# Down projection of a decode step: fourteen rows in row form, fourteen as stationary blocks, five loads in place of four

## The chip, the cores and the metric

The kernel runs on one core of one Trainium2 chip. The metric is the device time of one execution in microseconds (us). Every number of a "time" below is such a device time; numbers with a place in the execution ("at 404.6") are counted from the start of the profiled span, which is about 1.8 us shorter than the device time. PE is TensorE, DVE is VectorE, ACT is ScalarE, PSUM is the accumulator memory that PE writes.

## The reference

One token goes through attention over a cache of 65,536 positions and then through a gated feed-forward layer. Only the last product matters here.

```python
def _B_ref(x, w_gate, w_up, w_down):
    return (_gelu(x @ w_gate) * (x @ w_up)) @ w_down     # F = 3584, D = 1024, one row of x

h  = x + _A_ref(_layernorm(x), ...)                      # attention, [cut]
h2 = h + _B_ref(_layernorm(h), w_gate, w_up, w_down)
```

The down projection multiplies a vector of 3584 values by a 3584 x 1024 matrix of bf16 (7.3 MB). The kernel splits the 3584 as 128 partitions x 28, so there are 28 "rows" c, each of 128 x 1024 weights. 1024 outputs are 8 x 128 (index j, then p).

## The kernel before

Two ways of forming the products stand in it. In **row form** the activations are stationary, padded to 32 columns, and the weights stream by, 512 columns at a time. The sums come out as rows, in four bands of a PSUM bank. They then need a copy to SBUF (`d_r`) and a product with a selector (`cp_sum`) that turns them into columns. In **masked form** the stationary operand has 8 columns, of which only column j is not zero, and 128 weight columns stream by; each product then adds into row j of an 8 x 128 result, which needs no turning.

```python
def pair_mm(bank, stat, w2, c, first, last):                   # row form
    for s in range(DS):                                        # DS = 2
        g = 2 * s + c % 2
        nc.tensor.matmul(bank[32 * g:32 * g + 32, :], lhsT=stat, rhs=w2[:, s * 512:(s + 1) * 512],
                         start=first, stop=last, tile_position=(0, 32 * g))

def cp_sum(row, add, name):                                    # rows to columns, plus add
    ps = ps_t.tile([P, 4, DS], F32, name=name + "_ps", tag="T")
    for b in range(4):
        nc.tensor.matmul(ps[:, b, :], lhsT=row[:, b * P:(b + 1) * P], rhs=hsel[:], start=True, stop=True)
    # [cut: one DVE add of ps and add]

# [cut: attention, out projection, layer norm, gate and up projections, which leave act_bf]
sizes = [FC // 2, FC // 2 - 5, 4, 1]                           # 14, 9, 4, 1 rows
NW = sizes[0] + sizes[1]                                       # 23 rows in row form
actz = padded(rows, act_bf[:, 0:NW], NW, "actz")
# [cut: actm, the masked stationary operands, filled by 8 copies]

c0 = 0
for sz in sizes[:2]:
    wv = load(wd_v[:, c0:c0 + sz, :], "wd_sb")
    for cc in range(sz):
        c = c0 + cc
        pair_mm(d_ps, actz[:, c, :], wv[:, cc, :], c, c < 2, c + 2 >= NW)
    c0 += sz
d_r = rows.tile([P, 512], F32, name="d_r")
nc.vector.tensor_copy(out=d_r[:], in_=d_ps[:])
wv = load(wd_v[:, c0:c0 + sizes[2], :], "wd_sb")
masked_rows(wv, c0, True, False)                               # 4 rows x 8 masked products
c0 += sizes[2]
hd_cp = cp_sum(d_r, h_cp, "hd_cp")
nc.tensor.matmul(o_ps[:], lhsT=hd_cp[:], rhs=ident_f[:], start=False, stop=False)
wv = load(wd_v[:, c0:c0 + sizes[3], :], "wd_sb")
masked_rows(wv, c0, False, True)                               # the last row
o_row = rows.tile([DC, P], BF16, name="o_row")
nc.vector.tensor_copy(out=o_row[:], in_=o_ps[:])
nc.sync.dma_start(out=out[0, 0].rearrange("(c p) -> c p", p=P), in_=o_row[:])
```

## Time and profile before

| | before |
|---|---|
| median of 3 executions | 419.05 us (418.85 to 419.56) |
| the profiled execution | 417.21 us, span 415.4 |
| read from HBM | 173.02 MB, 416 GB/s over the span |
| start of the down projection's products (`d_ps`) | 399.13 |
| end of the last weight packets | 407.4 |
| end of `o_row`, after which only the store is left | 413.33 |

The page of the profile cuts the span into 40 equal slices. The rows below are the granted clock of TensorE in tenths of full speed, the busy share of the DMA engines in tenths, and what they moved. The load stream is full until the last slice.

```profile
span 415.4 us, 6247 instructions
...
PEclk9997999999899999599999967999999586658866
DMA  8999999999999999999999999999999999999990
GB/s 354 429 429 437 420 447 420 437 433 428 443 420 402 431 439 428 433 422 432 437 428 429 434 432 428 420 422 437 431 429 438 423 440 426 430 436 423 434 409 32
```

The chain of waits, in order of time (start, length, what): followed back from the last instruction, what released each step.

```profile
376.18 28.39 DMA wd_sb<-in_B_w_down_dram
...
404.61 1.59 PE d_ps L358 x18
...
406.22 0.70 DVE d_r L471
...
406.96 1.86 PE hd_cp_ps L387 x8
408.82 3.50 PE o_ps L459 x32
412.33 0.23 PE o_ps L476 x2
412.56 0.46 PE o_ps L459 x8
...
413.05 0.28 DVE o_row L480
```

From the landing of the 9-row load on, PE and DVE work one after the other for 8.8 us without waiting for a load. The row form's closing (copy and column sum, 2.6 us) stands in the middle of it, and the 40 masked products behind that.

Stretches of half a microsecond of the same execution: length, PE busy (instructions), granted clock, DMA share, GB/s. The count in brackets includes instructions that only reach into the stretch, so length over count is not the distance between two starts.

```profile
401.50:402.00 0.50, 0.50 (x8) 0.50 0.83 356
402.00:402.50 0.50, 0.22 (x4) 1.00 1.15 492
...
405.50:406.00 0.50, 0.50 (x6) 0.50 0.39 160
...
407.00:407.50 0.50, 0.50 (x3) 0.50 0.04 16
```

The loads are over at about 407.4, six microseconds ahead of the end of `o_row`. The clock is 1.0 in one stretch of about 3.4 us (402.0 to 405.4) and 0.5 on either side.

### The profile page before, as it was taken

How to read it: one execution, taken by the hardware profiler on the slowest of the kernel's cores; microseconds unless marked ns; L12 is line 12 of the kernel's file. 1: busy time of each engine (PE TensorE's matmuls, PEld its weight loads, DVE VectorE, ACT ScalarE, POOL GpSimd, SP SyncE). 2: the span in 40 equal slices, each digit the busy share in tenths (PEclk: the TensorE clock that was granted, in tenths of full speed). 3: DMA queues.
4: the chain of work that ended last, by engine and by line, in shares of the span. 5: the costliest groups of instructions: out<-in, count | busy, mean ns of one | idle time of the engine just before them, and what ended most of it. 6: DMA issues, size and time to landing. Idle time of an engine off the chain costs nothing.

```text
span 415.4 us, 6247 instructions
## 1 busy us (share of the span) xinstructions
PE 302.2 (73%) x2652; PEld 196.9 (47%) x2652; DVE 168.2 (40%) x298; ACT 168.1 (40%) x281; POOL 5.7 (1%) x17
## 2 busy tenths in 40 slices
PE   0458989888788986597988929888986563575536
PEld 0227656564465664464565517465564231352215
DVE  0213565656356455354465526455465000011101
ACT  0014757545755653734565544365562700000000
POOL 1100000000000000000000000000000002000000
PEclk9997999999899999599999967999999586658866
DMA  8999999999999999999999999999999999999990
GB/s 354 429 429 437 420 447 420 437 433 428 443 420 402 431 439 428 433 422 432 437 428 429 434 432 428 420 422 437 431 429 438 423 440 426 430 436 423 434 409 32
DMA packets 6684, 173.43 MB, mean 417 GB/s; under 512 B 896, under 2 KB 896, under 8 KB 1152
## 3 DMA queue, kind: packets, MB, share of 16 engines
q1 hardware_dynamic: 6496, 173.02, 97.2%
q8 instruction: 21, 0.34, 0.3%
q14 instruction: 7, 0.06, 0.0%
q10 hardware_dynamic: 160, 0.00, 0.0%
HBM read 173.02 MB, written 0.00 MB: 416 GB/s over the span
## 4 chain that ended last, share of the span: by engine, by line
PE 51%; DMA 20%; DVE 13%; issue 8%; ACT 6%; POOL 1%; SPq 0%; POOLq 0%; ACTq 0%; DVEq 0%
PE kt_ps L220 27%; PE qk_ps L245 11%; DMA k_sb<-in_A_k_cache_dram 7%; DMA wd_sb<-in_B_w_down_dram 7%; DMA v_sb<-in_A_v_cache_dram 6%; DVE sc_sb L256 5%; PE acc_ps L300 5%; PE sct_ps L253 4%; ACT pT L283 4%; DVE mx L257 3%; DVE kt_sb L227 3%; ACT qk_sb L250 2%; PE wg_ps L160 1%; PE o_ps L459 1%; PE o_ps L316 1%
## 5 line engine op out<-in xcount | busy, mean ns | idle before, releaser
L220 PE MATMUL kt_ps<-ident_f,k_sb 128*128 128x128 f32 x1024 | 149.2, 289 | 15.9 <-DVE kt_sb L227 13.0
L225 ACT COPY kt_sb<-kt_ps 128x1024 bf16<-128x1024 bf16 x116 | 116.4, 1013 | 91.7 <-PE kt_ps L220 61.6
L220 PEld LDWEIGHTS kt_ps<-ident_f,k_sb 128*128 128x128 f32 x1024 | 118.2, 147 | 53.9 <-issue 21.2
L227 DVE COPY kt_sb<-kt_ps 128x1024 bf16<-128x1024 bf16 x140 | 94.8, 687 | 74.5 <-PE qk_ps L245 41.9
L245 PE MATMUL qk_ps<-kt_sb,qsel 128*32 128x512 bf16 x512 | 65.4, 397 | 7.3 <-DVE kt_sb L227 7.3
L256 DVE COPY sc_sb<-sct_ps 128x512 f32<-128x512 f32 x32 | 34.2, 1067 | 47.3 <-PE sct_ps L253 45.0
L283 ACT ACTIVATE pT<-sc_sb,nbias 128x256 bf16<-128x256 f32 x64 | 31.5, 494 | 20.4 <-DVE nbias L275 20.4
L300 PE MATMUL acc_ps<-v_sb,pT 128*32 128x512 bf16 x512 | 33.7, 408 | 2.8 <-DMA v_sb<-in_A_v_cache_dram 2.8
L250 ACT COPY qk_sb<-qk_ps 128x512 f32<-128x512 f32 x32 | 18.9, 590 | 24.8 <-PE qk_ps L245 16.5
L245 PEld LDWEIGHTS <-qsel 128*32 128x32 bf16 x512 | 15.1, 94 | 26.7 <-issue 24.4
L253 PE MATMUL sct_ps<-ident_f,qk_sb 128*128 128x128 f32 x128 | 20.4, 283 | 8.6 <-ACT qk_sb L250 8.6
L300 PEld LDWEIGHTS <-pT 128*32 128x32 bf16 x512 | 14.3, 101 | 18.0 <-issue 6.2
L257 DVE TENSOR_REDUCE mx<-sc_sb 128x8 f32<-128x512 f32 x32 | 22.0, 686 | 1.0
L253 PEld LDWEIGHTS sct_ps<-ident_f,qk_sb 128*128 128x128 f32 x128 | 14.7, 143 | 13.6 <-ACT qk_sb L250 13.6
L167 ACT COPY wg_ev<-wg_ps 96x512 f32<-96x512 f32 x1 | 0.6, 582 | 45.6 <-PE wg_ps L160 45.6
L309 PE MATMUL l_ps<-lpart,ones_f 128*128 128x8 f32 x16 | 3.7, 306 | 15.6 <-ACT pT L283 15.6
L358 PE MATMUL at_ps<-wo_sb,o2z 128*32 128x512 bf16 x64 | 7.2, 629 | 9.4 <-DMA wo_sb<-in_A_wo_dram 9.4
L160 PEld LDWEIGHTS <-hnz 128*32 128x32 bf16 x112 | 5.0, 125 | 15.3 <-issue 13.3
L167 ACT ACT_TABLE_LOAD x1 | 1.3, 1283 | 26.9 <-DVE q_ev L165 26.9
L160 PE MATMUL wu_ps<-wu_sb,hnz 128*32 128x512 bf16 x56 | 6.7, 597 | 7.4 <-DMA wu_sb<-in_B_w_up_dram 7.4
L283 ACT ACTIVATION_READ_ACCUMULATOR pT<-sc_sb,nbias 128x1 f32 x64 | 12.0, 187 | 0.0
L309 PEld LDWEIGHTS l_ps<-lpart,ones_f 128*128 128x128 f32 x16 | 3.0, 234 | 17.8 <-ACT pT L283 17.4
(126 smaller groups left out, 103.0 us busy)
## 6 DMA issues: line engine op xcount, KB each, us to landing
k_sb<-in_A_k_cache_dram SPq DMA_DIRECT2D x16, 4096.0 KB, 26.6
v_sb<-in_A_v_cache_dram SPq DMA_DIRECT2D x16, 4096.0 KB, 21.6
wq_sb<-in_A_wq_dram SPq DMA_DIRECT2D x2, 4096.0 KB, 17.0
wo_sb<-in_A_wo_dram SPq DMA_DIRECT2D x2, 4096.0 KB, 28.8
wg_sb<-in_B_w_gate_dram SPq DMA_DIRECT2D x2, 3584.0 KB, 32.4
wu_sb<-in_B_w_up_dram SPq DMA_DIRECT2D x1, 3584.0 KB, 41.2
wd_sb<-in_B_w_down_dram SPq DMA_DIRECT2D x1, 3584.0 KB, 25.1
wu_sb<-in_B_w_up_dram SPq DMA_DIRECT2D x1, 2688.0 KB, 37.8
```

Source lines behind the costliest of these rows:

```text
L160: nc.tensor.matmul(banks[s // 4][32 * g:32 * g + 32, :], lhsT=stat, rhs=mov(s), start=first, stop=last, tile_position=(0, 32 * g))
L220: nc.tensor.transpose(out=kt_ps[:, b, :], in_=k32s[m0 // 16][:, m0 % 16, :], identity=ident_f[:])
L225: nc.scalar.copy(out=dst_bf, in_=src_bf)
L227: nc.vector.tensor_copy(out=dst_bf, in_=src_bf)
L245: nc.tensor.matmul(qk_ps[32 * c:32 * c + 32, :], lhsT=qsel[:, g, par, hf, :], rhs=mv[:, :, :, par], start=(hf == 0 and par == 0), stop=(hf ...
L250: nc.scalar.copy(out=qk_sb[:], in_=qk_ps[:])
L253: nc.tensor.transpose(out=sct_ps[:, b, :], in_=qk_sb[:, b * P:(b + 1) * P], identity=ident_f[:])
L256: nc.vector.tensor_copy(out=sl.rearrange("p h (m t) -> p m t h", t=2), in_=src_v)
L257: nc.vector.tensor_reduce(out=st["mx"][:, :, pi], in_=sl, axis=AX.X, op=ALU.max)
L283: nc.scalar.activation(out=pT[:, :, r, :], in_=sc_sb[:, r, hf * HG * TG:(hf + 1) * HG * TG].rearrange("p (a t) -> p a t", t=TG), func=ACT. ...
L300: nc.tensor.matmul(acc[32 * c:32 * c + rep * TG, :], lhsT=pTs[a // HG][:, a % HG, :, :].rearrange("p r t -> p (r t)"), rhs=v_sb[:, i * TG: ...
L358: nc.tensor.matmul(bank[32 * g:32 * g + 32, :], lhsT=stat, rhs=w2[:, s * 512:(s + 1) * 512], start=first, stop=last, tile_position=(0, 32 ...
```

## The change

The intent is to have less work behind the last byte. Only the first 14 rows keep the row form, so its closing can run while loads still come. The other 14 rows turn the product round: a 128 x 128 block of weights is stationary and one column of activations streams by, so the sums come out as columns at once. One add and one transpose close the sum. The last loads get smaller: 7, 4, 2 and 1 rows.

```diff
-    sizes = [FC // 2, FC // 2 - 5, 4, 1]
-    NW = sizes[0] + sizes[1]
+    sizes = [14, 7, 4, 2, 1]
+    NW = sizes[0]
     actz = padded(rows, act_bf[:, 0:NW], NW, "actz")
-    [cut: actm, its 8 copies, o_ps, masked_rows]
+    dl_ps = ps_w.tile([P, DC], F32, name="dl_ps", tag="w")
+    nc.vector.memset(dl_ps[:], 0.0)
     c0 = 0
-    for sz in sizes[:2]:
+    for sz in sizes:
         wv = load(wd_v[:, c0:c0 + sz, :], "wd_sb")
         for cc in range(sz):
             c = c0 + cc
-            pair_mm(d_ps, actz[:, c, :], wv[:, cc, :], c, c < 2, c + 2 >= NW)
+            if c < NW:
+                pair_mm(d_ps, actz[:, c, :], wv[:, cc, :], c, c < 2, c + 2 >= NW)
+                continue
+            for j in range(DC):
+                nc.tensor.matmul(dl_ps[:, j:j + 1], lhsT=wv[:, cc, j * P:(j + 1) * P], rhs=act_bf[:, c:c + 1],
+                                 start=False, stop=False, skip_group_check=True)
         c0 += sz
-    [cut: d_r, 4 masked rows, cp_sum, the product of hd_cp and ident_f, the last masked row]
+        if c0 == NW:
+            d_r = rows.tile([P, 512], F32, name="d_r")
+            nc.vector.tensor_copy(out=d_r[:], in_=d_ps[:])
+            hd_cp = cp_sum(d_r, h_cp, "hd_cp")
+    h2_cp = rows.tile([P, DC], F32, name="h2_cp")
+    nc.vector.tensor_tensor(out=h2_cp[:], in0=dl_ps[:], in1=hd_cp[:], op=ALU.add)
+    h2T_ps = ps_t.tile([DC, P], F32, name="h2T_ps", tag="T")
+    nc.tensor.transpose(out=h2T_ps[:], in_=h2_cp[:], identity=ident_f[:])
     o_row = rows.tile([DC, P], BF16, name="o_row")
-    nc.vector.tensor_copy(out=o_row[:], in_=o_ps[:])
+    nc.vector.tensor_copy(out=o_row[:], in_=h2T_ps[:])
```

More of the change, by code (lines that the diff above doesn't have):

```diff
@@ L443 @@
     wd_v = B_w_down.rearrange("(p c) n -> p c n", p=P)
-    sizes = [FC // 2, FC // 2 - 5, 4, 1]
-    NW = sizes[0] + sizes[1]
-    NM = FC - NW
+    sizes = [14, 7, 4, 2, 1]
+    assert sum(sizes) == FC
+    NW = sizes[0]
     actz = padded(rows, act_bf[:, 0:NW], NW, "actz")
-    actm = rows.tile([P, NM, DC * DC], BF16, name="actm")
-    nc.gpsimd.memset(actm[:], 0.0)
-    for j in range(DC):
-        nc.vector.tensor_copy(out=actm[:, :, j * (DC + 1)], in_=act_bf[:, NW:FC])
     d_ps = row_bank("d_ps")
-    o_ps = ps_w.tile([DC, P], F32, name="o_ps", tag="w")
-    def masked_rows(wv, c0, first, last):
-        n = wv.shape[1]
-        for cc in range(n):
-            for j in range(DC):
-                nc.tensor.matmul(o_ps[:], lhsT=actm[:, c0 + cc - NW, j * DC:(j + 1) * DC],
-                                 rhs=wv[:, cc, j * P:(j + 1) * P], start=(first and cc == 0 and j == 0),
-                                 stop=(last and cc == n - 1 and j == DC - 1))
+    dl_ps = ps_w.tile([P, DC], F32, name="dl_ps", tag="w")
+    nc.vector.memset(dl_ps[:], 0.0)
     c0 = 0
-    for sz in sizes[:2]:
+    for sz in sizes:
         wv = load(wd_v[:, c0:c0 + sz, :], "wd_sb")
@@ L467 @@
             c = c0 + cc
-            pair_mm(d_ps, actz[:, c, :], wv[:, cc, :], c, c < 2, c + 2 >= NW)
-        c0 += sz
-    d_r = rows.tile([P, 512], F32, name="d_r")
-    nc.vector.tensor_copy(out=d_r[:], in_=d_ps[:])
-    wv = load(wd_v[:, c0:c0 + sizes[2], :], "wd_sb")
-    masked_rows(wv, c0, True, False)
-    c0 += sizes[2]
-    hd_cp = cp_sum(d_r, h_cp, "hd_cp")
-    nc.tensor.matmul(o_ps[:], lhsT=hd_cp[:], rhs=ident_f[:], start=False, stop=False)
-    wv = load(wd_v[:, c0:c0 + sizes[3], :], "wd_sb")
-    masked_rows(wv, c0, False, True)
+            if c < NW:
[4 more added lines that the diff above has]
+                                 start=False, stop=False, skip_group_check=True)
+        c0 += sz
+        if c0 == NW:
[6 more added lines that the diff above has]
+    nc.tensor.transpose(out=h2T_ps[:], in_=h2_cp[:], identity=ident_f[:])
     o_row = rows.tile([DC, P], BF16, name="o_row")
-    nc.vector.tensor_copy(out=o_row[:], in_=o_ps[:])
+    nc.vector.tensor_copy(out=o_row[:], in_=h2T_ps[:])
     nc.sync.dma_start(out=out[0, 0].rearrange("(c p) -> c p", p=P), in_=o_row[:])
```

## The prediction

> **What bounds the kernel.** For most of the span the load stream does: the slices show DMA at 0.9 or more, 173 MB at 417 GB/s. The change touches only the end. The chain of waits follows the down-projection loads until 404.56, where the 9-row load lands and releases PE. From there it is PE and DVE without a gap: row matmuls 1.6 us, copy d_r 0.7, its sum to columns 1.9, the 40 masked matmuls 3.5 and 0.5 (the residual product 0.2 between), copy o_row 0.28, done at 413.33; the span ends at 415.4. Yet the DMA packets end at 407.4 (the stretches show almost no traffic after 407). So 6 us of serial work lie behind the last load.
>
> **What the change removes, adds, moves.**
> - The 9-row load becomes 7 rows: 512 KB (1.2 us at about 420 KB/us) come later; the end of the stream stays at 407.4. The loads should land near 403.4, 405.9, 407.1 and 407.4.
> - d_r and its column sum need only the first 14 rows, whose matmuls ended at 402.2 in the timeline. They now run from 402.2 to about 404.1: 3 us leave the chain.
> - 18 row matmuls, the residual product and 40 masked matmuls (107 ns apart at clock 0.5, 56 ns at 1.0) go. 14 x 8 = 112 pairs of a 128x128 bf16 weight load and a one-column matmul come.
> - Cost of a pair: the only 128-column bf16 weight loads in the trace are esel and osel; their matmuls start 25 ns apart at clock 1.0. The f32 ones of that width (cp_sum) start 213 ns apart at 0.5[...].[...] I estimate 25 ns warm and, scaled like the f32 pair, 50 ns cold: 112 pairs cost 3 to 6 us, mostly hidden under the loads.
> - The clock: after the 3.5 us of one-column products hc_ps (busy throughout) the granted clock fell to 0.5, so such products seem not to hold it up. I assume 0.5 from about 405.4.
> - The new end is serial: add (0.17 us, as hd_cp), f32 transpose of 8 columns (0.38, as mxT at the slow clock, plus weight load), copy 0.28; with hops about 1.0 us.
> - 8 actm copies (0.66 us) and a memset go; PE was waiting for the load until 399.1 then: worth nothing.
>
> **Sum.** Four rows start at 405.9: 32 x 50 ns, to 407.5; two rows to 408.3; the last to 408.7, drained at 408.9. Add, transpose, copy: 409.9 instead of 413.3. Gain about 3.4 us, 0.8%: **415.6 us, range 413.8 to 418.2**. Faster by over 2%: 0.02; within 2%: 0.96; slower by over 2%: 0.02. Nothing here can give 2% (8.4 us): only 6 us lie behind the last byte.
>
> **What would show it.** Right: d_r copied near 402.3; stationary pairs 25 to 55 ns apart; PE stops within 2 us of the last landing; o_row ends near 410; packets still end near 407.4; nothing before 399 moves. Wrong: pairs 100 ns or more apart at clock 0.5; or cp_sum holding up the 7-row load's pairs; or later landings because smaller loads stretch the stream.
>
> **What would make it wrong.** If a pair costs about 110 ns at the slow clock[...], 90 pairs from 405.4 end near 415 and the change loses 3 us. If the clock stays at 1.0, PE finishes right after the last landing and the gain is 4.5 us. If the small loads cost extra, 0.5 us goes.

The forecast's sum runs over 32 pairs at 50 ns, two rows, the last row and the close to 409.9, a gain of 3.4 us, and so to 415.6 us. The 50 ns stand as my estimate, doubled from the 25 ns measured at clock 1.0.

## The result, and the profile after

The changed kernel took 412.72 us (median of 4 executions, 412.36 to 413.13), the kernel before 418.95 us (418.75 to 419.56) on the same occasion. The ratio is 0.985, with a 95% interval of 0.983 to 0.987. It is the mean time of one kernel's fast executions over that of the other's of the same rounds, so it is not quite the ratio of the medians. The gain is 6.2 us where 3.4 were forecast, and the time lies below the forecast range.

The profiled execution after (412.36 us): slices and chain of waits.

```profile
span 410.5 us, 6349 instructions
...
PEclk9986999999999999599999966999999585568565
DMA  8999999999999999999999999999999999999994
```

```profile
372.76 25.63 DMA wd_sb<-in_B_w_down_dram
...
398.43 3.20 PE d_ps L358 x28
...
401.66 0.70 DVE d_r L465
...
402.40 1.86 PE hd_cp_ps L387 x8
404.27 3.06 PE dl_ps L460 x112
...
407.35 0.18 DVE h_cp L468
...
407.57 0.39 PE h2T_ps L470
...
407.99 0.28 DVE o_row L472
```

The chain no longer passes through the small loads. It leaves the load stream at the landing of the first 14 rows and is PE and DVE work from there to the end: row products, copy, column sum, and all 112 block products in one piece of 3.06 us.

The timeline of the block products (start, length, then weight load or product, operands and shapes, count), and two stretches of half a microsecond in them:

```profile
403.92 3.31 PEld L460 LDWEIGHTS <-wd_sb 128*128 128x128 bf16 x112
404.13 3.19 PE L460 MATMUL dl_ps<-act_bf,wd_sb 128*128 128x1 bf16 x112
```

```profile
404.50:405.00 0.50, 0.50 (x25) 0.50 0.53 209
...
406.50:407.00 0.50, 0.50 (x23) 0.50 0.00 0
```

One product lasts 165 ns from start to end, and they overlap: (3.19 - 0.165) / 111 = 27 ns from one start to the next. PE is never idle among the 112, although the granted clock is 0.5 throughout. The forecast had 50 ns at this clock.

I call the stretch from the start of `d_ps` to the end of `o_row` the **tail**. It fell from 14.20 us (399.13 to 413.33) to 9.84 us (398.43 to 408.27).

### The profile page after: what moved, and what is told of

It reads as the page before. It is cut to its first block, busy times and chain, and to the rows that moved or that the text cites. A ratio compares the mean times of both kernels' runs of the same rounds, so it can differ in the third digit from the quotient of the medians.

```text
span 410.5 us, 6349 instructions
## 1 busy us (share of the span) xinstructions
PE 297.7 (73%) x2705; PEld 195.3 (48%) x2705; DVE 167.6 (41%) x292; ACT 168.0 (41%) x281; POOL 5.1 (1%) x16
## 4 chain that ended last, share of the span: by engine, by line
PE 51%; DMA 20%; DVE 14%; issue 8%; ACT 6%; POOL 0%; SPq 0%; POOLq 0%; ACTq 0%; DVEq 0%
PE kt_ps L220 26%; PE qk_ps L245 11%; DMA k_sb<-in_A_k_cache_dram 7%; DMA wd_sb<-in_B_w_down_dram 6%; DMA v_sb<-in_A_v_cache_dram 6%; DVE sc_sb L256 5%; PE acc_ps L300 5%; ACT pT L283 4%; PE sct_ps L253 4%; DVE mx L257 4%; DVE kt_sb L227 3%; ACT qk_sb L250 2%; PE o_ps L316 1%; PE wg_ps L160 1%; PE d_ps L358 1%
## 5 line engine op out<-in xcount | busy, mean ns | idle before, releaser
L253 PEld LDWEIGHTS sct_ps<-ident_f,qk_sb 128*128 128x128 f32 x128 | 14.3, 140 | 13.6 <-ACT qk_sb L250 13.6
L283 ACT ACTIVATION_READ_ACCUMULATOR pT<-sc_sb,nbias 128x1 f32 x64 | 11.9, 187 | 0.0
```

The costliest lines, as they stand in the source:

```text
L253: nc.tensor.transpose(out=sct_ps[:, b, :], in_=qk_sb[:, b * P:(b + 1) * P], identity=ident_f[:])
L283: nc.scalar.activation(out=pT[:, :, r, :], in_=sc_sb[:, r, hf * HG * TG:(hf + 1) * HG * TG].rearrange("p (a t) -> p a t", t=TG), func=ACT. ...
```

## The experiments

All variants gave correct results. Kernels that were sent together ran on the same chip and share their executions of the kernel before.

### Both kernels again: c_before and c_after

No edit. They are to tell whether the surplus gain lies in the tail or ahead of it.

> The kernel before again, as a null run and to get its trace on this chip. If the surplus of the gain over the forecast (6.2 us measured, 3.4 forecast) lies wholly behind the last load, its profile repeats the first one: 14.2 us from the start of d_ps (landing of the 14-row load) to the end of o_row, and d_ps starting near 399.1. If part of the surplus is difference between executions before the tail, the start of d_ps moves by about 1 us from the first profile and the stretch from there stays 14.2 us. Ratio to before 1.000 +- 0.002.

> The changed kernel again. Theory A (cheap block pairs and early closing, all behind the 14-row landing): from d_ps start to o_row end 9.8 us again, against 14.2 of before, 4.4 us of gain whatever the rest of the execution does; ratio about 0.985 to 0.989. Theory B (something ahead of the tail got faster through the change): d_ps starts earlier than in c_before by 1 us or more, also here on the same chip.

Measured: c_before 417.89 us (416.56 to 418.64, 6 executions), ratio 0.999. c_after 412.28 us (412.23 to 412.43, 4 executions), ratio 0.986 (0.984 to 0.989). In the traces the tails repeat: 14.25 us before, 9.83 after. The products `d_ps` start at 398.41 in c_before and at 398.39 in c_after. So nothing ahead of the tail got faster through the change, and theory B falls: the 0.7 us by which the first two profiles differ at that point is a difference between executions. The other profiles bear this out: over all 13 that are not slow the first products of the down projection start between 398.37 and 399.48, early and late ones among the variants of either kernel.

That leaves a riddle. The profiled executions of the kernel before are 417.21 and 416.56 us, but the medians of the kernel before are 417.8 to 419.05: the first profile is faster than all timed executions of its set (418.85 and up), the second is the fastest of its own six.

### The form alone, and the split alone: e_st23 and e_mk14

e_st23 keeps before's loads and its 23 rows in row form; the last 5 rows are blocks.

```diff
 (against the changed kernel)
-    sizes = [14, 7, 4, 2, 1]
-    NW = sizes[0]
+    sizes = [14, 9, 4, 1]
+    NW = sizes[0] + sizes[1]
```

> Only the form of the last 5 rows changed: before's loads (14, 9, 4, 1) and 23 rows in row form, the last 5 as stationary blocks, closed by add and transpose. Theory A: PE still waits for the 9-row load (5.4 us after the 14-row one), then row matmuls 1.6, d_r 0.7, column sum 1.9, then 40 pairs at 27 ns = 1.1 instead of 4.2 us of masked matmuls, then 1.1 us of add, transpose and copy instead of 0.3: from d_ps start to o_row end about 12.0 us, 2.2 us better than before, ratio 0.995. If the pairs were slow when few (50 ns or more), 13 us or more.

e_mk14 has the changed kernel's loads and its early closing, and the other 14 rows in masked form.

```diff
 (against the kernel before)
-    sizes = [FC // 2, FC // 2 - 5, 4, 1]
-    NW = sizes[0] + sizes[1]
+    sizes = [14, 7, 4, 2, 1]
+    NW = sizes[0]
 ... first load: pair_mm, then d_r and cp_sum at once; other loads: masked_rows;
 ... the product of hd_cp and ident_f ahead of the last load's masked rows
```

> Only the split and the loads changed: after's loads (14, 7, 4, 2, 1) and 14 rows in row form, but the other 14 rows by the masked matmuls of before (112 of them). Theory A: the early closing alone is worth nothing with this form, since 112 masked matmuls at 107 ns until the clock rises and 56 ns after it need 9 to 12 us after the column sum ends 5.9 us behind d_ps start: 15 to 18 us to the end of o_row, ratio 1.002 to 1.010. If the early closing were the main gain, 11 to 12 us and ratio 0.993.

Measured: e_st23 414.78 us (413.94 to 415.74), ratio 0.992 (0.990 to 0.995). Its tail is 12.43 us (398.42 to 410.85), near the 12.0 expected; the row products of the 9-row load took 2.32 us instead of 1.6. From its timeline:

```profile
403.86 2.32 PE L358 MATMUL d_ps<-wd_sb,actz 128*32 128x512 bf16 x18 [2.27 <-DMA wd_sb<-in_B_w_down_dram]
...
408.69 1.21 PE L460 MATMUL dl_ps<-act_bf,wd_sb 128*128 128x1 bf16 x40
```

The 40 block products take 1.21 us; the 40 masked ones they replace took 4.2 us. The few pairs are as cheap as the many: (1.21 - 0.165) / 39 = 27 ns from one start to the next.

The profiled execution of e_mk14 fell in a slow state that lasted the whole execution (568.3 us, PE busy 501 us of 566); what slowed it is not known, and it is left out. The other five lie between 414.48 and 419.23 us, median of all six 417.29, ratio 0.997 (0.993 to 1.0005). I had expected 1.002 to 1.010, so the masked form did better than that. It was profiled again, as one look:

> The split kernel with masked matmuls again, since its profiled execution was in the slow state. Its fast executions spread from 414.5 to 419.2 us. Theory C: the spread is that of the 112 masked matmuls over the clock's phase, 107 ns apart at 0.5 and 56 at 1.0, so from the end of the column sum to the end of o_row between 8 and 11 us, and the start of d_ps stays within 398.4 to 399.5.

Measured: 417.79 us, tail 14.39 us (399.40 to 413.79), and 8.56 us of it from the end of the column sum (405.23) to the end of `o_row`. Its timeline and stretches (PE busy, granted clock, DMA share, GB/s):

```profile
405.17 7.64 PE L459 MATMUL o_ps<-wd_sb,actm 128*8 128x128 bf16 x104
```

```profile
405.20:407.00 1.80, 1.80 (x19) 0.50 0.36 142
407.00:409.00 2.00, 2.00 (x24) 0.57 0.02 8
409.00:411.00 2.00, 2.00 (x40) 1.00 0.03 8
```

About 3.5 us after the start of the dense masked products (at 408.7, as the mean of 0.57 over the second stretch gives) the clock rises, and their starts, 107 ns apart until then, come 56 ns apart. This is within what the second expectation gave, and it says why the first was too high: the clock rose sooner.

What follows from the two: the split alone is worth 0.3%, not clearly more than nothing. The form alone is worth 0.8%. Together they give 1.4% to 1.5%. The tails point the same way: with block products the early closing and its loads took 12.43 us (e_st23) down to 9.84. With masked ones it took the tail of 15.53 us in c_before3 (below), which starts at the same 399.40, to 14.39, and there the clock rose. So closing the row form early seems to pay most if what comes behind it is short, which the block form makes it. The intervals of the two ratios are too wide to exclude that the two gains simply add.

### What a block pair costs: e_half and e_half2

Each block is cut into two of 64 columns; the products are the same.

```diff
-                nc.tensor.matmul(dl_ps[:, j:j + 1], lhsT=wv[:, cc, j * P:(j + 1) * P], rhs=act_bf[:, c:c + 1], ...)
+                for s in range(2):
+                    nc.tensor.matmul(dl_ps[64 * s:64 * s + 64, j:j + 1],
+                                     lhsT=wv[:, cc, j * P + 64 * s:j * P + 64 * s + 64], rhs=act_bf[:, c:c + 1],
+                                     ..., tile_position=(0, 64 * s))
```

> The changed kernel with each stationary block cut into two of 64 columns: 224 pairs in place of 112, the same products. Theory A1[...], 224 x 53 = 11.9 us in place of 3.1, so the end of o_row comes about 8.8 us later, ratio about 1.007. Rival A2 (27 ns is a cost per issued pair whatever the width): 224 x 27 = 6.0 us, about 3 us later, ratio about 0.993. Rival A3 (cost follows the width): 14 ns each, no change, ratio 0.986.

(Theory A1 was based on 53 ns for a half block; the two runs below measure it.)

Measured: 415.62 us (415.25 to 416.58), ratio 0.995 (0.992 to 0.997), 224 products in one piece of 6.14 us. That is the number of A2, 27 ns per pair issued. But the start times show more: the two halves of a block start together, within 3 ns, and the next two 53 ns later. So this run did not settle it: it may be 27 ns for each, or 53 ns with two side by side in different columns of the array. e_half2 puts all left halves of a load first and then all right ones, so that neighbours share their columns.

> As e_half, but in each load all the left halves first and then all the right ones, so that neighbouring pairs use the same columns of the array. In e_half the two halves of a block started 3 ns apart and the next couple 53 ns after, so it did not tell a cost per pair from loads that run side by side. Theory A1 ([...]53 ns at the slow clock, and e_half hid one behind the other): 53 ns from pair to pair, 224 x 53 = 11.9 us from the first block pair to the last, the end of o_row about 15.5 to 16 us... no less than 18 us behind the start of d_ps, ratio 1.005 to 1.01. Rival A2 (27 ns for any pair issued): 6.0 us as in e_half, ratio 0.994.

Measured: 420.83 us (420.36 to 422.44), ratio 1.009 (1.005 to 1.013). Here are the two timeline lines, of e_half and of e_half2:

```profile
405.25 6.14 PE L461 MATMUL dl_ps<-act_bf,wd_sb 128*64 128x1 bf16 x224
```

```profile
404.60 10.80 PE L463 MATMUL dl_ps<-act_bf,wd_sb 128*64 128x1 bf16 x224
```

The starts are 53 ns apart at clock 0.5, except for a few pairs at each of the seven changes from left to right halves and back, where they come closer; that is why the 224 take 10.8 us and not 11.9. (The expectation's two figures for the tail contradict each other, which was my slip. Measured: 17.5 us.) So a half block takes 53 ns and a full block 27. The half blocks differ from the full ones in `tile_position` as well as in width, and no run tells which of the two makes the difference.

The forecast had taken the 25 ns of the `esel` blocks at clock 1.0 and doubled it. In the timeline of the kernel before this is the line

```profile
29.82 0.20 PE L185 MATMUL qsel_ps<-qT_bf,esel 128*128 128x32 bf16 x2 [0.28 <-DVE qT_bf L182]
```

(two products of 176 ns with 32 columns each; in the trace their starts are 25 ns apart, and so are those of the four `osel` products). In the trace of the changed kernel both groups fell in stretches at clock 0.5. There the `esel` starts (at 27.91) are 25 ns apart and the `osel` ones (at 343.73) 26 to 28. So the pairs that the forecast doubled took the same at either clock, within 3 ns. What sets this distance is not shown: no block product of any run here ran at clock 1.0, and no run takes its causes apart. What is shown is 25 ns at clock 1.0 (`esel`, `osel`), and at 0.5 25 to 28 ns (the same) and 27 (the blocks).

### Is more to be had: v_all and v_pc

v_all makes all 28 rows blocks; row form, `d_r` and column sum go, and `h_cp` is added at the end.

```diff
-            if c < NW:
-                pair_mm(...)
-                continue
             for j in range(DC): (block products, as before)
-        if c0 == NW: (d_r, cp_sum)
-    nc.vector.tensor_tensor(out=h2_cp[:], in0=dl_ps[:], in1=hd_cp[:], op=ALU.add)
+    nc.vector.tensor_tensor(out=h2_cp[:], in0=dl_ps[:], in1=h_cp[:], op=ALU.add)
```

> All 28 rows as stationary blocks, no row form, no d_r, no column sum; loads as in the changed kernel. Theory A: 224 pairs at 27 ns are 6 us, 3 of them under the 14-row load's successor, so PE is never behind the loads for long and ends 0.5 us after the last landing (packets end 8.15 us behind d_ps start in the changed kernel): o_row ends about 9.5 us after the first landing instead of 9.8, ratio 0.985 to 0.986, hardly better than the changed kernel. If the pairs were the bound, worse.

Measured: 412.62 us (412.31 to 413.81), ratio 0.988 (0.985 to 0.990), the same as the changed kernel within the noise, in a different session. Its tail is 9.88 us (398.67 to 408.55), where about 9.5 was expected. Its timeline shows the landings, because PE now waits for each (in brackets: the idle time before and what ended it).

```profile
398.67 3.15 PE L454 MATMUL dl_ps<-act_bf,wd_sb 128*128 128x1 bf16 x112 [4.85 <-DMA wd_sb<-in_B_w_down_dram]
...
402.92 1.65 PE L454 MATMUL dl_ps<-act_bf,wd_sb 128*128 128x1 bf16 x56 [1.09 <-DMA wd_sb<-in_B_w_down_dram]
...
405.38 1.01 PE L454 MATMUL dl_ps<-act_bf,wd_sb 128*128 128x1 bf16 x32 [0.81 <-DMA wd_sb<-in_B_w_down_dram]
...
406.61 0.99 PE L454 MATMUL dl_ps<-act_bf,wd_sb 128*128 128x1 bf16 x24 [0.22 <-DMA wd_sb<-in_B_w_down_dram]
```

The landings come 4.25, 6.7 and 7.9 us behind the first, and the last row's products start 8.56 us behind it (at 407.23, after a short gap inside the last group). The forecast had 4.3, 6.8, 8.0 and 8.3. In the changed kernel PE reaches the last row 8.5 us behind the first landing (404.13 + 104 x 0.027 - 398.43), which is as early as v_all's last load let it start. So its tail can hardly get shorter by faster products.

v_pc takes every eighth column into a block, so that a partition ends with 8 neighbouring outputs; the transpose, the copy and `cp_sum` go.

```diff
 (against v_all)
-                nc.tensor.matmul(..., lhsT=wv[:, cc, j * P:(j + 1) * P], ...)
+                nc.tensor.matmul(..., lhsT=wv[:, cc, j::DC], ...)
-    (add into h2_cp, transpose, copy to o_row)
+    nc.vector.tensor_tensor(out=h2_pc[:], in0=dl_ps[:], in1=h_pc[:], op=ALU.add)       # bf16
+    nc.sync.dma_start(out=out[0, 0].rearrange("(p c) -> p c", c=DC), in_=h2_pc[:])
```

> As v_all, but the blocks take every eighth column, so that the sums come out with 8 neighbouring outputs in each partition: the residual is the column form that the layer norm already has, and the transpose and the copy go; the add writes bf16 and the result leaves as 128 runs of 16 bytes instead of 8 of 256. If strided blocks load as fast as packed ones (25 to 30 ns a pair): the store starts about 0.75 us earlier than in v_all, ratio about 0.9835.[...]

Measured: 416.48 us (416.37 to 417.24), ratio 0.997 (0.9945 to 0.999), 3.9 us slower than v_all:

```profile
398.37 13.62 PE L443 MATMUL dl_ps<-act_bf,wd_sb 128*128 128x1 bf16 x224 [5.28 <-DMA wd_sb<-in_B_w_down_dram]
```

```profile
399.40:400.40 1.00, 1.00 (x20) 0.50 0.97 414
...
409.40:410.40 1.00, 1.00 (x20) 0.50 0.00 0
```

(In the second fence: length of the stretch, PE busy, granted clock, DMA share, GB/s.) The starts are 60 ns apart at clock 0.5, not the 25 to 30 ns expected in case strided blocks load as fast as packed ones. A pair with a stationary block of strided columns took more than twice the 27 ns of a packed one at the same clock, and PE, not the loads, is then what bounds the end. No version that beats the changed kernel was found.

### Where the rest of the gain comes from: e_wbefore, c_before2, c_before3

The tail of the kernel before consists of products whose pace follows the clock (107 ns at 0.5 against 56 at 1.0 for a masked one; for the 18 row products 2.32 us at 0.5, in c_before3, against 1.26 at 1.0, in e_wbefore). Of these the tail after keeps only the first row products, and beside them the column sum. Theory C says that the median of before holds tails longer than the two profiled. The first attempt was to hold the clock up with useless products.

```diff
 (against the kernel before)
         wv = load(wd_v[:, c0:c0 + sz, :], "wd_sb")
+        if c0 == 0:
+            filler(9, actz[:].rearrange("p c k -> p (c k)")[:, 0:512])     # 512-column products, result unused
         for cc in range(sz): ... pair_mm(...)
+        if c0 == 0:
+            filler(6, wv[:, 0, 0:512])
```

> The kernel before with 9 useless 512-column matmuls in the idle time ahead of the down projection's first row matmuls and 6 in the wait for the 9-row load, to hold the granted clock at 1.0 in the tail. Theory C (the tail of before depends on the clock's phase, and its usual execution is 1 to 2 us worse than the profiled one for that reason): with the clock at 1.0 the masked matmuls go 56 ns apart and the column sum takes 0.95 us, the tail from d_ps start to o_row end falls from 14.2 to about 11.5 us and the ratio to 0.990 to 0.993, and its executions lie within 1 us of each other, unlike the 3 us of before. Rival (the spread of before comes from ahead of the tail): tail shorter, but the spread stays at 2 to 3 us.

Measured: 417.15 us (414.42 to 418.14), ratio 0.997 (0.994 to 1.0001). The profiled tail is shorter, 12.97 us: the clock was 1.0 for most of the first row products (1.95 us) and for the 18 later ones, but it fell at 407.03, within the column sum (1.30 us against 1.86 before) and ahead of the masked products, and the first 32 of them took 3.29 us, nearly as without fillers. So the clock was not held where it was meant to be, and the spread did not shrink (3.7 us). A shorter tail with the old spread is what the rival had foretold. With the clock held only in part, this is no fair test of theory C.

So the kernel before was profiled twice more.

> The kernel before once more, for another profiled execution: the two profiled so far (417.21 and 416.56 us) are the fastest of their sets, whose medians are about 418. Theory C: the tail (d_ps start to o_row end, 14.2 in both) depends on the clock's phase; an execution of 417.5 us or more shows a tail of 14.9 to 15.4 us, with the 18 row matmuls of the 9-row load taking 2.3 instead of 1.3 to 1.6 us at clock 0.5. Rival: the tail stays 14.2 and the extra time lies before the start of d_ps (398.4 to 399.1 so far), which would come at 399.5 or later.

> The kernel before, a third profiled execution of it, for the same question as c_before2. Theory C: an execution of 417.5 us or more has a tail of 14.9 to 15.4 us from the start of d_ps to the end of o_row. Rival: tail 14.2, start of d_ps at 399.5 or later.

Measured: c_before2 took 416.85 us and c_before3 418.9 us; the latter is an execution like the medians. Timeline lines of c_before3:

```profile
399.40 3.18 PE L358 MATMUL d_ps<-wd_sb,actz 128*32 128x512 bf16 x28 [5.57 <-DMA wd_sb<-in_B_w_down_dram]
404.86 2.32 PE L358 MATMUL d_ps<-wd_sb,actz 128*32 128x512 bf16 x18 [2.28 <-DMA wd_sb<-in_B_w_down_dram]
...
413.56 1.06 PE L459 MATMUL o_ps<-wd_sb,actm 128*8 128x128 bf16 x8
```

| execution of before | time | start of d_ps | 18 row products | last 8 masked | tail |
|---|---|---|---|---|---|
| first profile | 417.21 | 399.13 | 1.57 | 0.61 | 14.20 |
| c_before | 416.56 | 398.41 | 1.26 | 0.86 | 14.25 |
| c_before2 | 416.85 | 398.37 | 1.25 | 1.06 | 14.45 |
| c_before3 | 418.9 | 399.40 | 2.32 | 1.06 | 15.53 |

In the three faster ones the clock is 1.0 for about 3.4 us behind the first row products; in c_before3 it is 0.5 for the whole tail. Stretches over the 18 row products, of the first profile and then of c_before3, and over the last products of c_before3:

```profile
404.60:406.20 1.60, 1.57 (x18) 0.75 0.56 228
...
404.80:407.20 2.40, 2.32 (x18) 0.50 0.42 172
...
412.00:414.70 2.70, 2.62 (x23) 0.50 0.02 6
```

The tail is 1.3 us longer than in the first profile, most of it in the 18 row products (2.32 against 1.57 us). Theory C and its rival both hold a part: the start of `d_ps` also moves, by 1.0 us between these executions. The second part is ahead of the change. What causes it stays open; it is met in the changed kernel too, whose four executions of the first set have spans of 410.5 and 411.2, two each.

The two parts may hang together. In these traces the granted clock changes only on a grid of 3.41 us steps, which lies differently in each (in the first profile of the kernel before, for one, at 402.00, 405.41 and 412.24; in that of the changed kernel at 393.01 and 396.43). In the three faster executions the first row products filled 2.86, 3.18 and 2.76 us of one step, and the clock was 1.0 from the end of that step. In c_before3, where they start later, they filled 2.33 us, and the clock stayed at 0.5. In the two profiles of the changed kernel they are split over two steps (at most 1.95 us in one), and the clock is 0.5 in the whole tail. How much a step was filled does not tell all: in v_pc PE was busy with one-column products for 13.6 us without a pause, and the granted clock was 0.50 in every stretch of it, while in e_mk14b it rose after about 3.5 us of masked products, and in c_before3 4.9 us of them saw it stay at 0.50. All this was read from the traces afterwards, and no run tests it.

The spreads of whole sets do not settle more. Kernels with block products and no masked ones spread by 0.2 to 1.5 us (after, c_after, e_half, v_all, v_pc), but e_st23 by 1.8 and e_half2 by 2.1; the kernel before by 2.1 to 3.0 us in the three later sets, but by 0.8 in the first set of four; e_wbefore by 3.7; the fast executions of e_mk14, with 112 masked products, by 4.8. This fits theory C on the whole, and it is not a test of it.

## Why the prediction was wrong

**What held.** The gain lies where it was placed: in the tail, by less work behind the last load. The row form closes early (`d_r` at 401.66, 3.2 us behind the start of `d_ps`, as forecast), the landings came as forecast to 0.3 us (as far as v_all shows them), the end of the packets moved only with the rest of the execution, and the close by add, transpose and copy took 0.95 us (forecast 1.0). The removal of the `actm` copies was not tested alone; in both profiles PE waited for the first load after that point, as forecast.

**The step that failed** is the one that the forecast put as "25 ns warm and, scaled like the f32 pair, 50 ns cold", and the term of the sum "Four rows start at 405.9: 32 x 50 ns, to 407.5; two rows to 408.3; the last to 408.7". The clock was 0.5 there as assumed, but a pair cost 27 ns. Block products ended 8.9 us behind the start of `d_ps` instead of 9.8. This happened in spite of a second miss of opposite sign: the forecast counted on clock 1.0 up to about 405.4, but it was 0.5 in the whole tail, so the column sum took 1.86 us and ended 0.9 us later than forecast. The scaling was carried over from the f32 pair, which does go from 112 ns at clock 1.0 (column sum of e_wbefore) to 213 at 0.5; the bf16 pairs took 25 ns at full clock (`esel`, `osel`) and 25 to 28 at half (the same, and 27 for the blocks). Why they do not follow the clock is not shown. The tail gained 14.20 - 9.84 = 4.36 us and not 3.43. By itself this miss makes 0.9 us: 419.05 - 4.36 = 414.7, which is still 2 us above the time measured.

**The second failure** is in the base, not in the change, and it is the larger: of the 2.8 us of surplus gain (6.23 - 3.43) the tail makes 0.9, and what the sum below lists beside the tail makes 1.9, most of it the base (1.38). The forecast subtracted a gain, worked out in one execution of 417.21 us, from a median of 419.05. The 1.8 us between the two were taken as common to both kernels. They can be in part a tail at the slow clock (15.5 us, as c_before3 shows, against 14.2). The changed kernel's tail cannot be stretched that way: its two profiled tails, 9.84 and 9.83 us, ran at clock 0.5 from end to end.

The sum for the first pair of sets: tail 4.36; start of `d_ps` 0.70 earlier, by chance of the execution; store and the time outside the span -0.21; distance of the median from the profiled execution, 418.95 - 417.21 = 1.74 for before and 412.72 - 412.36 = 0.36 for after, so 1.38. That is 6.23, and the medians differ by 418.95 - 412.72 = 6.23. How the last 1.38 divides between the tail and the start of the tail in those very executions was not traced; c_before3 shows that each can give about 1 us. The range was too narrow below for want of both.

The warning in the forecast that a pair might cost 110 ns at the slow clock, about what a masked product took there (107), did not come true (27). e_half2, with 224 pairs at 53 ns, shows what it would have looked like.

## What to carry to other kernels

A duration measured at one clock need not scale to another: here an f32 pair went from 112 to 213 ns at half the clock, while bf16 pairs took 25 ns at full and 25 to 28 ns at half clock. Before scaling, ask what sets the distance between starts, and look for the same shape at the other clock. For a matrix times one vector, full and packed 128 x 128 bf16 blocks as the stationary operand cost 27 ns each even at the slow clock, give the sums as columns, and leave little work at the end that depends on the clock. When the profiled execution is faster than the median, find out what differs before subtracting a gain from the median: a change can remove the variable part too.
